# The Mixer's 128x640 turns by transposing transfers on ScalarE's queue instead of TensorE

## The chip, the cores and the metric

The kernel runs on one core of a Trainium2 chip. The metric is the device time of one execution in microseconds. Times of the kernel before come from three runs; the profile is of one execution, taken by the hardware profiler.

## The reference

Two layers are applied twice in turn to x, a sequence of 2048 tokens of width 640 (bf16): an attention layer A with recurrent memory, and a token mixer with an MLP, B.

```python
# A: for each segment of 32 tokens, with 8 memory rows in front
h = concat(mem, xs)                      # 40 x 640
q, k, v = h @ Wq, h @ Wk, h @ Wv         # 32 heads of 192
p = softmax(mask(q k^T * scale))
o = (p v) @ Wo
mem = o[:8]; out = o[8:]
# B
h  = gelu(layernorm(x) @ w1)             # 640 x 640
hs = shift the four quarters of h by +1, -1, +2, -2 tokens, @ w2
x1 = x + hs
out = x1 + gelu(layernorm(x1) @ w3) @ w4 # 640 x 1536, 1536 x 640
# the whole
x = x + A(layernorm(x)); x = x + B(layernorm(x))   # twice
```

The memory makes A serial over its 64 segments. Every weight is the same for both applications.

## The kernel before

**Tiling and stages.** Both layers run at the same time in two lanes: in step t lane 0 does segment t of the first A, lane 1 does segment t - 5 of the second (`LAG = 5`). There are 69 steps (`T_A`); steps 5 to 63 carry both lanes. A step goes through eight groups of four heads: `keys_queries` (L1707 on TensorE, copies out of PSUM at L1717, L1725, L1732), `values` or `values3` (L1754, L1781, copies L1742), `attend` (scores `fs` L1832, mask and minimum `f1` L1844, exponential L1851, sums and scaling L1855 to L1857, transposes of P L1867, copy `f5` to PT L1875, P V L1884, copy to oT L1892), and `project` (L1910). The step's result is copied from PSUM to `hT` of the next step (L1937) and, turned the feature way up, to `yTB` (`fy`, L1951, L1953). Most of the A weights are streamed from HBM in every step by SyncE (`load_pair`, L1565), the rest stay in SBUF.

**The Mixer.** B runs in 34 chunks of 64 tokens per lane, 128 rows together, a chunk over two steps: `chunk(c)` and `chunk_end(c)` belong to steps 2c + 2 and 2c + 3; the last chunk runs alone after the last step. A chunk goes through these operations, and three of them turn a 128x640 tile:

- turn one, `ft` (L2106): five TensorE transposes of `yTB` (features by tokens) into the PSUM tile `psx`; Vector adds the residual and writes `xw` (`fx`, L2111);
- LayerNorm (`ln_ops` L1964 to L1974, whose power is on GpSimd, and `apply_ln` L1980) into `vb`, which lies in the tile `vbg`;
- turn two, `transposes` (L1990): five transposes of `vb` into the PSUM tile `psv`; ScalarE copies it to `vT`, a view of `hTB` (`fe`, L2189), and four columns a second time to the end of `vT` for the lanes' neighbours (`fel`, L2192);
- w1 (L2217), GELU (`gelu`, L2008 to L2021), w2 (L2277), sums (`fs`, L2294), LayerNorm into `vb` again;
- turn three, `transposes` (L1990) and ScalarE's copy to `vT` (`fe3`, L2314);
- w3 (L2340), GELU, w4 (L2386), output `xo` (also in `vbg`, L2401) and the stores (L2425);
- `ft4` (L2440) and `fc` (L2448) hand the second A its input.

Between turn one and turn two another small product, `ftl` (L2171), prepares the next segments of the first A through the same `vb`.

**What sets the order.** Every operation is given to a planner with its engine, a cost in us, a due time and the buffers that it reads and writes (`Plan.add`). On each engine the operations stand in the order of a rank: a number from the table `RANK` for the kind of step or chunk, relative to the step's start in units of a nominal 48 us step, or, without a number there, the due time. `Plan.place` goes through the engines' lists by these ranks and its cost model, takes PSUM banks (classes A: six, B: two) and weight slots as they come free, and emits the instructions in that order; each engine's queue then runs in order, with the waits that the buffers need. A transfer's end is modelled from its size and a service rate, and SyncE's loads are also held back by the plan's time (`paced`).

Of the kernel before, what the change touches and what calls it, by code (L numbers as in the profile page):

```python
# [68 lines left out]
FLYING = 5  # L69

# [3 lines left out]
        "apply_ln.f": (390816740, 987286415, 2774608591, 3364870645,),  # L74
        "chunk.f1": (-18948399,),
        "chunk.f2": (-18747072,),
        "chunk.f3": (800691382,),
        "chunk.fe": (797633711,),
        "chunk.fe3": (3465816136,),
        "chunk.fel": (797835038,),  # L80
        "chunk.fhr": (1956035521,),
        "chunk.fhs": (3270088812,),
        "chunk.fk0": (-16266273,),
        "chunk.fk1": (1952815952,),
        "chunk.fs": (3364467992, 3364669318,),
        "chunk.ft": (18577175,),
        "chunk.ftl": (1090352636,),
        "chunk.fw": (1840327660, 1831464498, 1835801008, 3056417763, 2844233677, 2854672191, 3570130801,
            3466017462, 3490601037, 4126209402, 4046269944, 4151504855, 4600545815,),
        "chunk.fx": (31092176,),  # L90
        "chunk.fx0": (1294186538, 1072001195,),
        "chunk.fxu": (3507298104,),
# [6 lines left out]
        "load_b.fn": (-781700909, -673986775, -675212538, 1893151641, 1858630600, 1767371006, 2538152327,  # L99
            2634013608, 2675185310, 3536660548, 3527592540, 3694428291, 4147361095,),  # L100
        "transposes.f": (518350147, 3379279900,),
    },
    "chunk_0": {
        "apply_ln.f": (156241712, 835445425, 1938646249,),
        "chunk.f1": (-241661482433,),
        "chunk.f2": (-3501346185,),
        "chunk.f3": (171063840,),
        "chunk.fe": (172377420,),
        "chunk.fe3": (1969503562,),
        "chunk.fel": (172578747,),  # L110
        "chunk.fhr": (841729640,),
        "chunk.fhs": (1126117177,),
        "chunk.fk0": (941134134,),
        "chunk.fs": (1547467010, 1610110974,),
        "chunk.ft": (23776015,),
        "chunk.ftl": (171890876,),
        "chunk.fw": (256513716, 243923217, 243091367, 1428370183, 1347119499, 1346930792, 2056025287,
            1887285962, 2053039009, 2867104445, 3014371358, 2968972543, 3202475158,),
        "chunk.fx": (42023799,),
        "chunk.fx0": (367754743, 172569584,),  # L120
        "chunk.fxu": (1938774438,),
# [6 lines left out]
        "load_b.fn": (-170906047654, -170906047654, -170906047654, 920004857, 882220319, 896865883,  # L128
            1304411523, 1257239965, 1386097304, 2462708421, 2481349681, 2470811516, 2484920200,),
        "transposes.f": (164006783, 1639917844,),  # L130
    },
    "chunk_1": {
        "apply_ln.f": (3060163, 77375092, 1082267730, 1868642147,),
        "chunk.f1": (-13472039,),
        "chunk.f2": (-65645538,),
        "chunk.f3": (54909696,),
        "chunk.fe": (376700785,),
        "chunk.fe3": (2151782729,),
        "chunk.fel": (501333390,),
        "chunk.fhr": (1081898099,),  # L140
        "chunk.fhs": (2097828189,),
        "chunk.fk0": (-133135086,),
        "chunk.fk1": (993465105,),
        "chunk.fs": (1689125843, 1837451266,),
        "chunk.ft": (-11121120,),
        "chunk.ftl": (433773110,),
        "chunk.fw": (830339901, 876465320, 876266106, 1443901855, 1443901855, 1443901854, 2466889840,
            2660038962, 2340340861, 3074449991, 3356442335, 3074449991, 3363339559,),
        "chunk.fx": (-8037190,),
        "chunk.fx0": (594976846, 581135627,),  # L150
        "chunk.fxu": (2090344860,),
# [6 lines left out]
        "load_b.fn": (-1387119777, -1392412708, -1420538080, 1387323520, 1387320273, 1387321646, 1547275136,  # L158
            1584490728, 1570029792, 2481502538, 2596235860, 2552368796, 3225923724,),
        "transposes.f": (5504700, 1860426782,),  # L160
    },
    "chunk_2": {
        "apply_ln.f": (235355591, 231614731, 1557226389, 1715954030,),
        "chunk.f1": (-956916103,),
        "chunk.f2": (-402470832,),
        "chunk.f3": (394002459,),
        "chunk.fe": (316376284,),
        "chunk.fe3": (1959638099,),
        "chunk.fel": (369464748,),
        "chunk.fhr": (778257113,),  # L170
        "chunk.fhs": (1679713241,),
        "chunk.fk0": (646066165,),
        "chunk.fk1": (898552330,),
        "chunk.fs": (1715148724, 1715350050,),
        "chunk.ft": (57711930,),
        "chunk.ftl": (169733834,),
        "chunk.fw": (807022150, 806116800, 807023775, 1271841077, 1402935676, 1121619675, 2204982466,
            1956421294, 1956443760, 2937607038, 3058004067, 2968056114, 3969956053,),
        "chunk.fx": (70731042,),
        "chunk.fx0": (807216980, 804791840,),  # L180
        "chunk.fxu": (1766269180,),
# [6 lines left out]
        "load_b.fn": (-2760993007, -1565909139, -1546941875, 179913085, 793637071, 179914697, 1529941493,  # L188
            1521916561, 1529803044, 2359458277, 2313897850, 2415279936, 2436005180,),
        "transposes.f": (155739437, 1779757110,),  # L190
    },
    "chunk_end": {
        "apply_ln.f": (6227615410,),
        "chunk_end.fc": (6228018063, 6973159525, 6385136252,),
        "chunk_end.fs": (5865030923, 5870521714,),
        "chunk_end.fst": (5947665841, 6351475085,),
        "chunk_end.ft4": (6227816736,),
        "chunk_end.fw": (5037522785, 5655022894, 4980117654, 5161081694, 5762689724, 5693545930,),
        "chunk_loads.f": (5989782193, 6332049253, 6151745579, 6163156616, 6117879852,),
        "ln_ops.f1": (5947665841,),  # L200
        "ln_ops.f2": (6089632075,),
# [1132 lines left out]
def kernel(  # L1334
# [758 lines left out]
    def chunk(c):  # L2093
# [65 lines left out]
        if last:  # L2159
            warm(WARM[4], D(0.1), o0)  # L2160
# [149 lines left out]
        if last:  # L2310
            warm(WARM[12], D(0.55), o0)
# [239 lines left out]
```

## Time and profile before

| | us |
|---|---|
| median of 3 runs | 3194.13 (3189.72 to 3197.24) |
| profiled execution, first to last instruction | 3192.6 |
| TensorE busy (matmul) | 3085.9 (97%) |
| TensorE weight loads | 2758.7 (86%) |
| VectorE busy | 2050.3 (64%) |
| ScalarE busy | 1710.0 (54%) |
| GpSimd busy | 502.2 (16%) |
| granted TensorE clock, mean | 0.996 |
| moved by DMA | 859.45 MB, mean 269 GB/s |

The profiled execution's span lies inside the range of the three runs and 1.5 us below their median. "PE" is TensorE's matmul row and "PEld" its weight loads, which overlap; DVE is VectorE, ACT ScalarE, POOL GpSimd, SP SyncE. A row of groups shows line, engine, operation, what it writes and reads, how many, the busy time in us, the mean duration in ns, and how long the engine had been idle before it and for whom. Matmuls overlap, so a matmul's duration (some 220 ns for 128 columns) is not what it costs TensorE: that is the distance from one start to the next. The columns of an issue row are the size in KB and the median us from the issue to the landing.

### The profile page before, as it was taken

Reading aid. Unit: us, or ns where it says so; the run is one execution under the profiler, and the core shown is the slowest. Engines: PE = TensorE matmul, PEld = TensorE weight load, DVE = VectorE, ACT = ScalarE, POOL = GpSimd, SP = SyncE. Lnnn points to the kernel's source line nnn. Section 1 sums busy time; section 2 is a strip of 40 time slices with the busy share of each in tenths; the row PEclk is TensorE's granted clock in tenths of the full one; section 3 lists DMA queues with packets and bytes.
Section 4 is the critical chain, followed back from the end, with each engine's and each line's share of the span. In section 5 each row is a group of like instructions: output and inputs, shape, how many; then the busy total and the mean of one; then the engine's idle time right before and its main releaser. Section 6 shows DMA issues by size and latency. Waiting matters only on the chain. (4 is left out here: it accounts for less than half of the span.)

```text
span 3192.6 us, 158772 instructions
## 1 busy us (share of the span) xinstructions
PE 3085.9 (97%) x70199; PEld 2758.7 (86%) x70201; DVE 2050.3 (64%) x6448; ACT 1710.0 (54%) x3985; POOL 502.2 (16%) x983
## 2 busy tenths in 40 slices
PE   4899999999999999999999999999999999999998
PEld 3778889998888888888888889888898888888886
DVE  2666666666666666666666666666666666666675
ACT  1445555555555555565555555555555555555443
POOL 0001111111111111111111111111111111111000
PEclk8999999999999999999999999999999999999999
DMA  9888788887887887888788888877888888888786
GB/s 375 280 280 261 253 272 278 260 264 259 285 261 256 280 266 258 258 279 267 258 274 269 258 260 269 280 257 260 281 267 261 255 285 260 262 275 275 263 292 217
DMA packets 421674, 859.45 MB, mean 269 GB/s; under 512 B 48334, under 2 KB 216223, under 8 KB 420984
## 3 DMA queue, kind: packets, MB, share of 16 engines
q1 hardware_dynamic: 396776, 796.08, 75.9%
q0 software_dynamic: 24032, 53.12, 5.3%
q8 instruction: 550, 9.01, 1.2%
q14 instruction: 140, 1.15, 0.1%
q10 hardware_dynamic: 176, 0.09, 0.0%
HBM read 823.73 MB, written 25.37 MB: 266 GB/s over the span
## 5 line engine op out<-in xcount | busy, mean ns | idle before, releaser
L1707 PEld LDWEIGHTS <-wst 128*128 128x128 bf16 x19872 | 828.9, 99 | 89.4 <-issue 24.0
L1910 PE MATMUL psy<-oT,wo 128*128 128x80 bf16 (+1 forms) x16560 | 678.3, 200 | 6.9 <-issue 4.4
L1742 ACT CAST V<-psv 32x384 bf16<-32x384 f32 (+2 forms) x1032 | 478.4, 472 | 380.4 <-PE psv L1754 160.9
L1910 PEld LDWEIGHTS <-wo 128*128 128x128 bf16 x16560 | 618.0, 99 | 21.4 <-issue 19.2
L1707 PE MATMUL psk<-hT,wst 128*128 128x80 bf16 (+1 forms) x9936 | 560.6, 200 | 15.9 <-ACT hT L2448 7.1
L1707 PE MATMUL psq<-hT,wst 128*128 128x80 bf16 (+1 forms) x9936 | 541.2, 200 | 22.8 <-DMA wst<-in_A_Wq_dram 20.3
L1717 ACT CAST qT<-psq 128x480 bf16<-128x480 f32 (+1 forms) x552 | 293.6, 532 | 370.1 <-PE psq L1707 324.3
L1844 DVE CUSTOM_DVE_ANT_1 pss<-pss,mask 80x320 f32<-80x320 f32 (+2 forms) x552 | 258.5, 468 | 307.4 <-PE pss L1832 276.4
L1732 DVE CAST kT<-psk 64x160 bf16<-64x160 f32 (+1 forms) x1104 | 338.9, 307 | 93.8 <-PE psk L1707 50.8
L1892 ACT CAST oT<-pso 128x480 bf16<-128x480 f32 (+1 forms) x552 | 293.2, 531 | 176.0 <-PE pso L1884 151.2
L1851 ACT ACTIVATE Pm<-pss,sm 80x320 bf16<-80x320 f32 (+2 forms) x552 | 278.6, 505 | 162.6 <-DVE sm L1844 82.6
L1855 DVE TENSOR_REDUCE sm<-Pm 80x4 f32<-80x320 bf16 (+2 forms) x552 | 250.9, 454 | 118.9 <-ACT Pm L1851 109.6
L1875 ACT COPY PT<-pst 80x320 bf16<-80x320 bf16 (+2 forms) x552 | 220.2, 399 | 190.4 <-PE pso L1884 103.0
L1707 PE MATMUL psq<-hT,wq 128*128 128x80 bf16 (+1 forms) x6624 | 315.4, 200 | 5.8 <-issue 5.1
L1707 PE MATMUL psk<-hT,wk 128*128 128x80 bf16 (+1 forms) x6624 | 315.8, 200 | 2.1 <-issue 2.0
L1754 PEld LDWEIGHTS <-hT 128*128 128x128 bf16 x2320 | 206.5, 98 | 105.1 <-issue 1.4
L1754 PE MATMUL psv<-wv,hT 128*128 128x384 bf16 x1276 | 284.1, 326 | 0.8 <-ACT V L1742 0.8
L1857 DVE TENSOR_TENSOR Pm<-Pm,sm 80x320 bf16<-80x320 bf16 (+2 forms) x552 | 255.5, 463 | 44.3 <-PE pso L1884 0.5
L1707 PEld LDWEIGHTS <-wq 128*128 128x128 bf16 x6624 | 265.8, 99 | 17.5 <-issue 14.9
L1725 DVE CAST kT<-psk 128x320 bf16<-128x320 f32 (+1 forms) x552 | 253.4, 459 | 41.3 <-PE psk L1707 34.0
L1707 PEld LDWEIGHTS <-wk 128*128 128x128 bf16 x6624 | 266.7, 99 | 6.1 <-issue 5.8
L1762 POOL DMA_DIRECT2D vahead<-V x232 | 119.2, 515 | 954.0 <-ACT V L1742 719.5
(136 smaller groups left out, 4125.1 us busy)
## 6 DMA issues: line engine op xcount, KB each, us to landing
wst<-in_A_Wk_dram SPq DMA_DIRECT2D x556, 384.0 KB, 4.7
wst<-in_A_Wq_dram SPq DMA_DIRECT2D x556, 384.0 KB, 4.7
wstB<-in_B_w_dram SPq DMA_DIRECT2D x495, 320.0 KB, 4.5
wst<-in_A_Wv_dram SPq DMA_DIRECT2D x383, 384.0 KB, 4.9
wstB<-in_B_w_dram SPq DMA_DIRECT2D x132, 160.0 KB, 4.0
vahead<-V POOLq DMA_DIRECT2D x232, 84.0 KB, 4.2
V<-vahead POOLq DMA_DIRECT2D x232, 84.0 KB, 4.6
wo<-in_A_Wo_dram SPq DMA_DIRECT2D x8, 960.0 KB, 11.9
```

What stands on the lines that cost most here:

```text
L1707: nc.tensor.matmul(out=o[:, cc, 0:W], lhsT=wv(kc, GW * j + cc * P, GW * j + (cc + 1) * P), rhs=h[:, kc, cw:cw + W], start=begin(pq), stop= ...
L1717: nc.scalar.copy(out=qT[G % QT_BUFS][:, :, c0:c0 + N], in_=T(pq)[:, :, off:off + N])
L1725: nc.vector.tensor_copy(out=k4[:, :, 0::3, c0:c0 + N], in_=p4[:, :, 0::2, off:off + N])
L1732: copy(out=k4[r0:r1, :, jj, c0:c0 + N], in_=p4[r0:r1, :, 1, off:off + N])
L1742: (nc.vector.tensor_copy if e == "DVE" else nc.scalar.copy)(out=v_part(*dst), in_=a_)
L1754: nc.tensor.matmul(out=T(bank)[:], lhsT=left[:, kc, :], rhs=wv(kc, GWH * b, GWH * (b + 1)), start=(kc == 0), stop=(kc == KC - 1))
L1844: nc.vector.tensor_tensor_reduce(out=o, in0=o, in1=maskt.unsqueeze(1).to_broadcast([NR, HG, N]), scale=-scale, scalar=3.0e38, op0=ALU.add, ...
L1851: nc.scalar.activation(out=Pb[0:NR, :, 0:N], in_=o, func=ACT.Exp, bias=sm_[0:NR, 0:1], scale=-1.0)
L1855: nc.vector.tensor_reduce(out=sm_[0:NR, 2:2 + HG], in_=Pb[0:NR, :, 0:N], axis=AX.X, op=ALU.add)
L1857: nc.vector.tensor_tensor(out=Pb[0:NR, :, 0:N], in0=Pb[0:NR, :, 0:N], in1=sm_[0:NR, 6:6 + HG].unsqueeze(2).to_broadcast([NR, HG, N]), op=A ...
L1892: nc.scalar.copy(out=o_[:, :, off:off + N], in_=T(pso)[:, :, 0:N])
L1910: nc.tensor.matmul(out=o[:, m, cw:cw + W], lhsT=wo[:, cc, m * P:(m + 1) * P], rhs=o_[:, cc, 0:W], start=st, stop=True, skip_group_check=True)
```

## The change

In all chunks but the last, the three turns become transfers that transpose, issued from ScalarE's queue. Turn one goes from `yTB` to `vb` and Vector's add reads `vb` instead of PSUM; turns two and three go from `vb` straight to `vT`, so that the two ScalarE copies go. The copy `fel` now reads `vT` and so waits for the transfer. The last chunk stays as it was.

The planner gets a field for an operation's latency: a turn holds ScalarE's queue for `XT_HOLD` and is taken to have landed `XT_LAT2` after its start. `hTB` gets four more columns of two, the five statistics tiles become one tile, and the `RANK` tables are searched anew, at a finer unit: every order in the kernel changes. Of the tables, three rows of the new one are shown here, in units of 1/1099511627776 of the nominal us.

```diff
+XT_HOLD = 1.2
+XT_LAT = 3.0
+XT_LAT2 = 3.3
...
 RANK = {
     "chunk": {
...
-        "chunk.fe": (797633711,),
-        "chunk.fe3": (3465816136,),
...
-        "chunk.ft": (18577175,),
...
+        "chunk.fty": (-3046630172747,),
+        "chunk.fw": (14792287517455, 14867662951863, 14630708053172, 50076348630774, 49467729030636,
+            49681047132891, 59853592314991, 59856247135919, 59850937494063, 69405430859040, 60263937057968,
+            60798214861989, 72293677685014,),
...
+        "chunk.turn.fvt": (-2997552436766, 50057199061523,),
...
+        op.lat = lat
...
-        op.pr = round(67108864 * due) if k >= len(ranks) else round(67108864 * self.base) + ranks[k]
+        op.pr = round(1099511627776 * due) if k >= len(ranks) else round(1099511627776 * self.base) + ranks[k]
...
+            if o.lat:
+                done = s + o.lat
...
-    hTB = ctile([P, KC, TOK + 4, 2], bf16, "hTB")
+    hTB = ctile([P, KC, TOK + 8, 2], bf16, "hTB")
...
-    st4 = [ctile([P, 18], f32, f"st{i}") for i in range(5)]
+    st_all = ctile([P, 5 * 18], f32, "st")
+    st4 = [st_all[:, 18 * i:18 * i + 18] for i in range(5)]
...
-    nc.vector.memset(st4[4][:], 0.0)
+    nc.vector.memset(st_all[:], 0.0)
...
+        if last:
+            ps1 = ps(PB, [XB, KC, P], bf16, "psx")
+
+            def ft(op):
+                o = T(ps1)
+                for m in range(KC):
+                    nc.tensor.transpose(out=o[:, m, :], in_=yTB[:, m, 0:XB], identity=ident[:, :])
+            o0 = add("PE", mm_us(128, k=KC), D(0.05), ft, r=(B("yTB", 0), B("yTB", 1), B("fin")), w=(ps1,))
+        else:
+            def fty(op):
+                nc.scalar.dma_start_transpose(out=vb.rearrange("p (k f) -> p k f", k=KC), in_=yTB[:, :, 0:XB])
+            add("ACT", XT_HOLD, D(0.05), fty, r=(B("yTB", 0), B("yTB", 1), B("fin")), w=(vk,), dma=P * Dm * 2, lat=XT_LAT2)
 
         def fx(op):
-            nc.vector.tensor_tensor(out=xw[:], in0=T(ps1)[:].rearrange("p k f -> p (k f)"), in1=xres[:], op=ALU.add)
-        o1 = add("DVE", 0.49, D(0.05), fx, r=(ps1, B("xres")), w=(xk,))
+            in0 = T(ps1)[:].rearrange("p k f -> p (k f)") if last else vb
+            nc.vector.tensor_tensor(out=xw[:], in0=in0, in1=xres[:], op=ALU.add)
+        o1 = add("DVE", 0.49, D(0.05), fx, r=(ps1 if last else vk, B("xres")), w=(xk,))
...
+        def turn(due):
+            def fvt(op):
+                nc.scalar.dma_start_transpose(out=vT[:, :, 0:XB], in_=vb)
+            add("ACT", XT_HOLD, due, fvt, r=(vk,), w=(vTk,), dma=P * Dm * 2, lat=XT_LAT2)
+
         if last:
+            ps2 = tuple(ps(PB, [P, n_, XB], bf16, "psv") for n_ in (3, 2))
+            o0 = transposes(ps2, vb, XB, D(0.1), (vk,))
             warm(WARM[4], D(0.1), o0)
+        else:
+            turn(D(0.1))
...
-        def fe(op):
-            nc.scalar.copy(out=vT[:, :, 0:XB], in_=T(ps2)[:])
-
         def fel(op):
-            nc.scalar.copy(out=vT[:, :, XB:XB + 4], in_=T(ps2)[:, :, 0:4])
+            nc.scalar.copy(out=vT[:, :, XB:XB + 4], in_=vT[:, :, 0:4])
...
-            add("ACT", act_us(KC * XB), D(0.1), fe, r=(ps2,), w=(vTk,))
-            add("ACT", act_us(KC * 4), D(0.11), fel, r=(ps2,), w=(B("vTl"),))
+            add("ACT", act_us(KC * 4), D(0.11), fel, w=(vTk,))
...
-            add("ACT", act_us(KC * XB), D(0.55), fe3, r=(ps3,), w=(vTk,))
+            turn(D(0.55))
```

More of the change, by code (lines that the diff above doesn't have):

```diff
@@ L101 @@
-        "transposes.f": (518350147, 3379279900,),
+        "apply_ln.f": (-372675211020, 15218774534654, 47732342916953, 55180342874328,),
+        "chunk.f1": (-5297123625453,),
+        "chunk.f2": (-596251389129,),
+        "chunk.f3": (6474721953796,),
+        "chunk.fel": (8025093657600,),
+        "chunk.fhr": (23139865220247,),
+        "chunk.fhs": (45548344521130,),
+        "chunk.fk0": (-1407744258729,),
+        "chunk.fk1": (45517753037159,),
+        "chunk.fs": (48868920797077, 55126742107899,),
@@ L106 @@
[L106 to L118, printed above, removed]
@@ L160 @@
-        "transposes.f": (5504700, 1860426782,),
+        "apply_ln.f": (-8987776286037, -8986536832155, 11890397199987, 17337194053897,),
+        "chunk.f1": (-8987780203548,),
+        "chunk.f2": (-2820038147939457,),
+        "chunk.f3": (-8551644850071,),
+        "chunk.fel": (-4034404608917,),
+        "chunk.fhr": (-2686321409725761,),
+        "chunk.fhs": (16933861314027,),
+        "chunk.fk0": (-2820183299612071,),
+        "chunk.fk1": (-2753179778832609,),
+        "chunk.fs": (15076912177881, 15165530943066,),
@@ L768 @@
     },
     "start": {
[L770 to L779 removed]
+        "apply_ln.f": (-12485141366161404,),
@@ new lines @@
+        "chunk_loads.f": (-10676455869805473, -11687620307186189, -11687620307186188,),
+        "ln_ops.f1": (-12485143015423997,),
+        "ln_ops.f2": (-11687620307186190,),
+        "start.f1": (-12480908025790464,),
+        "start.f2": (-12480809814267804,),
+        "start.f3": (-12474469465651552,),
+        "start.f4": (-12485144664687195,),
+        "start.f5": (-12477688745721008, -12418499370294308, -12466767243769831, 91948283496292,),
+        "transposes.f": (-12480809814267805,),
@@ L1188 @@
     __slots__ = ("e", "d", "due", "fn", "n", "succ", "ready", "slots", "start", "end", "dma", "i", "margin",
-                 "paced", "last", "after", "mode", "pr")
+                 "paced", "last", "after", "mode", "pr", "lat")
 class Plan:
@@ L1203, in at, with add @@
         self.tag, self.base, self.seen = tag, base, {}
-    def add(self, e, d, due, fn, r=(), w=(), a=(), dma=0, queue=None, margin=0.0, after=(), mode=0, order=()):
+    def add(self, e, d, due, fn, r=(), w=(), a=(), dma=0, queue=None, margin=0.0, after=(), mode=0, order=(), lat=0.0):
         op = Op()
+        op.lat = lat
         op.mode = mode
@@ L2307, in chunk @@
         apply_ln(vb, uw, XB, st3, 0, vk, uk, s3k, D(0.5))
-        ps3 = tuple(ps(PB, [P, n_, XB], bf16, "psv2") for n_ in (3, 2)) if last else ps(PB, [P, KC, XB], bf16, "psv2")
-        o0 = transposes(ps3, vb, XB, D(0.55), (vk,))
         if last:
+            ps3 = tuple(ps(PB, [P, n_, XB], bf16, "psv2") for n_ in (3, 2))
+            o0 = transposes(ps3, vb, XB, D(0.55), (vk,))
             warm(WARM[12], D(0.55), o0)
-        def fe3(op):
-            nc.scalar.copy(out=vT[:, :, 0:XB], in_=T(ps3)[:])
-        if last:
             halves(ps3, D(0.55))
         else:
-            add("ACT", act_us(KC * XB), D(0.55), fe3, r=(ps3,), w=(vTk,))
+            turn(D(0.55))
         w3got = {}
```

1997 lines of the change are left out of this document (1137 added, 860 removed), and 150 rows, old and new, of the table RANK.

## The prediction

> **What bounds the kernel now.** I read the busy table and the window view first, then the rows of the three turns, then the order of time around two of them, then the issues of the transfers. The first two lines below are of the page, the third is the window view over one chunk (two steps) in mid-run; its columns are busy time of PE, weight loads, DVE, ACT and POOL, the granted clock, the DMA engines' share and GB/s.
>
> ```profile
> span 3192.6 us, 158772 instructions
> PE 3085.9 (97%) x70199; PEld 2758.7 (86%) x70201; DVE 2050.3 (64%) x6448; ACT 1710.0 (54%) x3985; POOL 502.2 (16%) x983
> ```
>
> ```profile
> 1585.00:1678.00 93.00, 92.47 (x2069) 83.49 (x2066) 61.70 (x192) 52.35 (x120) 17.60 (x34) 1.00 0.82 267
> ```
>
> TensorE is the bound: 92.47 of 93 us, at clock 1.00, while ACT is busy 52 of 93 us. So matmul time that goes is time gained, as long as TensorE doesn't wait for what replaces it.
>
> ```profile
> L1990 PE MATMUL psv<-ident,vbg 128*128 128x128 bf16 x340 | 30.3, 220 | 0.6 <-DVE vbg L1980 0.4
> ...
> L2189 ACT COPY hTB<-psv 128x640 bf16<-128x640 bf16 x33 | 22.9, 693 | 1.7 <-PE psv L1990 1.6
> L2314 ACT COPY hTB<-psv 128x640 bf16<-128x640 bf16 x33 | 22.8, 692 | 28.6 <-DVE xw L2305 22.2 <-PE psv L1990 6.3
> ...
> L2106 PE MATMUL psx<-ident,yTB 128*128 128x128 bf16 x170 | 15.1, 220 | 0.5 <-DVE yTB L1951 0.5
> ```
>
> The reader sees five transposes per turn, 99 turns outside the last chunk, and two ScalarE copies per chunk. (The two counts hold 5 and 10 of the last chunk.) The next rows are the order of time around turn one and turn two of one chunk (start, duration, engine).
>
> ```profile
> 1585.74 0.59 PE L1707 MATMUL psk<-hT,wst 128*128 128x80 bf16 x12 [0.26 <-ACT hT L2448]
> ...
> 1588.31 0.45 PE L2106 MATMUL psx<-ident,yTB 128*128 128x128 bf16 x5
> 1588.80 0.49 DVE L2111 TENSOR_TENSOR xw<-psx,xw 128x640 bf16<-128x640 bf16 x1 [1.39 <-PE psx L2106]
> 1589.90 0.87 DVE L1964 BATCH_NORM_STATS2 st<-xw 128x6 f32<-128x320 bf16 x2
> 1592.11 0.45 DVE L1980 TENSOR_SCALAR vbg<-xw,st 128x640 bf16<-128x640 bf16 x1 [0.44 <-POOL st L1974]
> 1592.73 0.45 PE L1990 MATMUL psv<-ident,vbg 128*128 128x128 bf16 x5
> ```
>
> The Mixer's first product (w1) starts only at 1607.93, 15 us after turn two: there was room in the chain. The third turn has none: w2 ends at 1625.35, its LayerNorm at 1628.70, the turn is at 1629.65 and w3 starts at 1631.00. What a transfer takes is seen in the issue list (KB, median us to landing).
>
> ```profile
> wst<-in_A_Wk_dram SPq DMA_DIRECT2D x556, 384.0 KB, 4.7
> wstB<-in_B_w_dram SPq DMA_DIRECT2D x132, 160.0 KB, 4.0
> h2u<-in_A_x_dram POOLq DMA_DIRECT2D x30, 80.0 KB, 2.5
> out_dram<-vbg POOLq DMA_DIRECT2D x30, 80.0 KB, 1.9
> ...
> ```
>
> **What goes.** Five transposes last 0.45 us and one 0.22, so each next one costs (0.45 - 0.22)/4 = 57 ns of TensorE. 99 turns x 5 x 57 ns = 28.2 us, all on the bound engine. About 1 us of TensorE's waits in front of these lines goes too. Sum: -29 us. [...]
>
> ScalarE loses 66 copies, 66 x 0.69 = 45.7 us, and gains 99 issues. Vector's add (0.49) reads SBUF instead of PSUM; the same operation with both inputs in SBUF (L2305) has 0.48, so nothing. The edge copy of 128x20 (0.19) stays, but now waits for the transfer. One tile for the five statistics tiles and four more columns in hTB touch only memsets at the start (under 0.4 us each): nothing. Two PSUM banks of class B lose three tiles a chunk; no wait for them is seen, so I count no gain.
>
> **What an issue and a landing cost.** The trace has no transposing transfer. The issue holds ScalarE's queue for between 0.33 us (an SP issue) and five such, 1.65 to 2.85 us (SP issues of 0.33 to 0.57), if it goes block by block. From issue to landing, L: at the least 1.7 us (0.33 plus what out_dram takes after its 0.57 us of issue, 1.33), at the most 6.5 (2.85 plus the 3.65 that the 160 KB load takes after its issue). The nearest row is the 160 KB load: the same bytes, a hardware queue, the same load on the engines, 4.0 us. A source in SBUF is worth some 0.6 less (1.9 against 2.5 for 80 KB). I take 3.4, with a spread of 0.8 both ways, since eight in ten of the weight loads behind the 4.0 landed between about 3 and 4.6. The plan itself assumes a hold of 1.2 and a landing of 3.3; that is what the order is built for, and no measurement.
>
> ScalarE's balance: 99 x 1.2 - 45.7 = +73 us, from 1710 to about 1783, 56%; at 0.33 it is -13, at 2.85 it is +236. In the window ScalarE has 40 us free per chunk, so as a sum it hides; what matters is what stands behind each issue in its queue. The 16.2 MB of the turns are 2% of 859 MB: DMA share 0.82 to about 0.84. SP issues as before, but its loads share the engines; the two long waits for weights (13.1 and 6.6 us) lie in the first 36 us, before any turn. POOL's queue loses and gains nothing; its stores of xo must now have left vbg before turn one writes it. The new ranks put those stores earlier, so nothing.
>
> **Where TensorE would wait.** The ranks fix each engine's order, so TensorE's work between two operations can be added up. As a check: by the old ranks there are 21.6 us between a chunk's first key matmul and w1, and the trace has 22.2.
>
> Turn one. By the new ranks, 23 units of six matmuls (0.215), 4 of eighteen (0.645), one value product (0.82) and one score product (0.28), 8.6 us, lie between the first key matmul and the second score product (attend.fs). That product needs a key copy which Vector runs behind the turn's consumers: add 0.49, key copy 0.31, statistics 1.37, mask 0.56, two key copies 0.66, LayerNorm 0.45, key copy 0.48, gaps 0.35 = 4.7 us. yTB is ready 0.5 us after the first key matmul. 0.55 + L + 4.7 + 0.07 = L + 5.3, against 8.6: TensorE waits for all of L beyond 3.3. Before, the turn cost 0.45 there. ScalarE stands likewise: turn two's issue waits for vb, with a query copy, the first PT copy and the second exponential behind it; the first output product needs that PT copy at 10.3 us. With a hold of 1.2 it comes at the same limit.
>
> Turn two. w1 is 15.3 us after the first key matmul, the issue at 8.0: room up to L = 7.0. The edge copy reaches the front of ScalarE's queue at about 13, so nothing waits below 5.
>
> Turn three. Between w2's end and w3 the new ranks leave 21 x 0.215 + 0.645 + 2 x 0.82 + 0.28 = 7.06 us. LayerNorm takes 3.35 (1625.35 to 1628.70 before), plus 0.1 for two semaphores: waits begin at L = 3.55. So the new order covers turns one and three up to about the planned landing of 3.3 us and no further; only turn two has room.
>
> Per chunk, with L of 2.6, 3.4 and 4.2 a third each: turn one (0 + 0.1 + 0.9)/3 = 0.33, turn three (0 + 0 + 0.65)/3 = 0.22; 0.55 x 33 chunks = 18 us. ACT and Vector run on meanwhile, so a wait for turn one is not paid again at turn two. The first chunks, where the page's first slices have the DMA engines at 0.9 and 0.8, I give 2 us more.
>
> **Sum.** 28.2 + 1 - 18 - 2 = 9 to 10 us less than the profiled execution's 3192.6 us of span, which lies 1.5 us below the median of 3194.13; the median less 10 is 3184. Half a step in L either way (0.2 us) moves this by some 7 us.
>
> **Rivals.**
> - Landings as the bulk of the weights have them, 4.2 to 4.7 us. For it: they share the engines at 0.82. Against it: ScalarE's queue has no backlog of its own. At 4.2, turn one 0.9 and turn three 0.65 (no spread): 51 us, 3194 - 29 + 51 = 3216; at 4.7, 1.4 + 1.15 = 2.55 x 33 = 84 us: 3249. It decides from L of about 3.8, where the 29 us are paid back. This is the case on the other side. Chance 0.29.
> - The gain and the waits cancel, L near 3.7 with the spread: 3188 to 3200. Chance 0.15.
> - The blocks go one after another: five issues of 0.57 and 3.65 after them, L = 6.5. Turn one 3.2, turn three 2.95, 6.15 x 33 = 203 us: 3368. For it speaks nothing in the trace but the size; chance 0.06. [...]
> - Landings of 2.6 or less: no waits, and all 29 us stay, 3165; with part of the 0.5 us a chunk that TensorE idles now in mid-run (93.00 - 92.47), 3155 to 3165. Chance 0.08.
>
> **How the numbers follow.** The likeliest case, L near 3.4, has 0.42: 3184, its own range 3165 to 3188. With the last rival it makes faster 0.50; same 0.15; slower 0.29 + 0.06 = 0.35. What a measurement here can tell from no change is 0.2%, 6.4 us. The range runs from 3160 (half of the small-L case, 0.04) to 3238 (L of 4.5: two thirds of the late-landing case, 0.19), with 0.42 and 0.15 between them: 0.80.
>
> **What would show it.** Right: the five-matmul rows of L2106 and L1990 shrink to 5 and 10 plus the start's; ScalarE's queue has three transposing issues a chunk; the issue list has 160 KB with a landing of 3 to 4 us; TensorE's waits for the mask, PT and hTB chains grow by about 0.5 us a chunk. Wrong: a median landing over 4, waits in front of w3 or of the second score product in every chunk, an issue that holds ScalarE for 2 us or more, or waits for weights in mid-run.

## The result and the profile after

The changed kernel takes 3391.69 us (median of 4 runs, 3369.08 to 3398.43), the kernel before on the same chip 3194.25 us (4 runs, 3189.72 to 3197.24). The ratio is 1.0606, 95% interval 1.0571 to 1.0641: 197 us slower, where 10 us faster was predicted and 3238 was the upper end of the range.

The first two lines are of the page of the changed kernel. The other two are the window view over some 2700 us in mid-run, in which both kernels start nearly the same number of products: first the kernel before, then the changed one (columns as in the prediction).

```profile
span 3396.7 us, 157771 instructions
PE 3137.8 (92%) x69703; PEld 2774.7 (82%) x69706; DVE 2057.8 (61%) x6448; ACT 1671.4 (49%) x3919; POOL 492.7 (15%) x983
```

```profile
300.00:2950.00 2650.00, 2625.73 (x58493) 2367.07 (x58491) 1739.80 (x5339) 1501.14 (x3396) 456.10 (x877) 1.00 0.82 267
```

```profile
310.00:3130.00 2820.00, 2675.03 (x58412) 2384.45 (x58411) 1756.98 (x5369) 1477.25 (x3358) 451.54 (x886) 0.99 0.85 257
```

TensorE has 496 products fewer, the 495 transposes among them, and takes 170 us longer over nearly as many: it was busy for all but 24 us of the first window and stood idle for 145 us of the second. The wait view of the changed kernel (total us, times, longest) says for whom, on TensorE and on Vector:

```profile
PE psh L2504 <- DMA hTB<-vbg: 65.4, 32, 5.9
PE pss L1991 <- DVE kT L1891: 51.0, 36, 3.5
...
PE pss L1991 <- DVE kT L1884: 11.7, 5, 3.0
```

```profile
DVE xw L2276 <- DMA vbg<-yTB: 57.9, 33, 5.6
DVE vbg L2336 <- DMA hTB<-vbg: 52.8, 23, 4.7
```

`psh` L2504 is w3: it waits for turn three in 32 of 33 chunks. The score products wait for key copies, and these stand on Vector behind the add of turn one (`xw` L2276), which waits 33 times for its transfer. Vector's second row is `f3`, its step of the small product `ftl`: it overwrites `vb` and so waits until turn two has read it. TensorE waits 0.6 us for it. The issue list has what the transfers took from issue to landing, which the trace before could not show, and the weights' loads beside them:

```profile
wst<-in_A_Wk_dram SPq DMA_DIRECT2D x556, 384.0 KB, 4.8
...
hTB<-vbg ACTq DMA_TRANSPOSE x66, 5.8
...
vbg<-yTB ACTq DMA_TRANSPOSE x33, 4.4
```

Here are both waits in one chunk, in order of time: turn one first, with ScalarE's issue, Vector's add and key copy, and TensorE's score product; then turn three.

```profile
1682.07 0.59 PE L1866 MATMUL psk<-hT,wst 128*128 128x80 bf16 x12 [0.26 <-ACT hT L2612]
...
1687.83 0.31 PE L1991 MATMUL pss<-kT,qT 128*128 128x80 bf16 x4
1690.09 0.30 PE L1991 MATMUL pss<-kT,qT 128*128 128x160 bf16 x2 [1.95 <-DVE kT L1891]
```

```profile
1682.22 1.22 ACTq L2271 DMA_TRANSPOSE vbg<-yTB  x1
```

```profile
1689.20 0.49 DVE L2276 TENSOR_TENSOR xw<-vbg,xw 128x640 bf16<-128x640 bf16 x1 [3.12 <-DMA vbg<-yTB]
1689.72 0.32 DVE L1891 CAST kT<-psk 64x160 bf16<-64x160 f32 x1
```

```profile
1727.94 1.22 ACTq L2324 DMA_TRANSPOSE hTB<-vbg  x1
```

```profile
1731.41 0.38 PE L1866 MATMUL psq<-hT,wst 128*128 128x80 bf16 x6
1733.25 1.56 PE L2504 MATMUL psh<-hTB,wstB 128*128 128x128 bf16 x25 [1.46 <-DMA hTB<-vbg]
```

Turn one is issued 0.15 us after the chunk's first key product and Vector can add 7 us later, the longest of the 33 (their mean is 5.0); TensorE runs out of work 1.95 us before the key copy is done. Turn three lands 5.3 us after its issue and w3 starts 1.46 us late. This chunk took 96 us where the one shown of before took 93.

To compare runs I add up TensorE's waits from the trace: of every distance between the starts of two successive products, what lies over the usual pitch of a product of its width (36 ns for 80 columns, 56 for 128; twice that where the granted clock is half, where the trace has 67 and 107), if it is more than 40 ns. "Clock" is the time lost to the granted clock by its records (in the changed kernel the mean is 0.979, and 3396.7 x 0.021 = 71). "On nothing shown" are the waits for which the trace has no releaser. All in us:

| run | span | clock | waits | on key copies | on turn three | on weights | on nothing shown | rest |
|---|---|---|---|---|---|---|---|---|
| before | 3193 | 13 | 150 | 4 | 0 | 25 | 50 | 71 |
| changed | 3397 | 71 | 329 | 82 | 71 | 34 | 39 | 103 |
| order_only | 3232 | 25 | 174 | 11 | 0 | 25 | 43 | 95 |
| nobody_waits | 3293 | 45 | 248 | 9 | 0 | 69 | 69 | 101 |
| unread_plain | 3200 | 19 | 152 | 3 | 0 | 27 | 48 | 74 |
| unread_transposing | 3236 | 21 | 187 | 6 | 0 | 30 | 81 | 70 |

From before to changed: 179 of waits, 58 of clock, less the 28 of the transposes, make 209; the spans differ by 204.

### The profile page after: what moved, and what is told of

The parts are those of the page before. It is cut to its first block, busy times and chain, and to the rows that moved or that the text cites. A ratio compares the mean times of both kernels' runs of the same rounds, so it can differ in the third digit from the quotient of the medians.

```text
span 3396.7 us, 157771 instructions
## 1 busy us (share of the span) xinstructions
PE 3137.8 (92%) x69703; PEld 2774.7 (82%) x69706; DVE 2057.8 (61%) x6448; ACT 1671.4 (49%) x3919; POOL 492.7 (15%) x983
## 3 DMA queue, kind: packets, MB, share of 16 engines
q8 instruction: 545, 8.93, 1.1%
## 4 chain that ended last, share of the span: by engine, by line
PE 69%; DMA 20%; DVE 7%; issue 2%; ACT 1%; POOL 0%; SPq 0%; DVEq 0%; POOLq 0%; ACTq 0%
PE psy L2069 15%; PE psk L1866 11%; DMA hTB<-vbg 10%; PE psq L1866 10%; PE psv L1913 10%; DMA vbg<-yTB 5%; PE pso L2043 4%; PE pss L1991 3%; PE psh L2504 3%; PE y L2550 3%; DMA wst<-in_A_Wq_dram 3%; PE psv L1940 2%; PE pst L2026 2%; PE psv L1971 2%; PE psh L2385 2%
## 5 line engine op out<-in xcount | busy, mean ns | idle before, releaser
L2069 PE MATMUL psy<-oT,wo 128*128 128x80 bf16 (+1 forms) x16560 | 692.8, 200 | 14.3 <-issue 7.4
L1901 ACT CAST V<-psv 128x384 bf16<-128x384 f32 (+3 forms) x1032 | 483.3, 475 | 405.5 <-PE psv L1913 284.3
L2069 PEld LDWEIGHTS <-wo 128*128 128x128 bf16 x16560 | 631.2, 99 | 43.1 <-issue 31.6
L1866 PE MATMUL psk<-hT,wst 128*128 128x80 bf16 (+1 forms) x9936 | 545.8, 200 | 14.1 <-ACT hT L2612 7.2
L1991 PE MATMUL pss<-kT,qT 128*128 128x80 bf16 (+2 forms) x3312 | 246.2, 211 | 67.0 <-DVE kT L1891 51.0
```

Source lines behind the costliest of these rows:

```text
L1866: nc.tensor.matmul(out=o[:, cc, 0:W], lhsT=wv(kc, GW * j + cc * P, GW * j + (cc + 1) * P), rhs=h[:, kc, cw:cw + W], start=begin(pq), stop= ...
L1901: (nc.vector.tensor_copy if e == "DVE" else nc.scalar.copy)(out=v_part(*dst), in_=a_)
L1991: nc.tensor.matmul(out=o[0:m_, i * N:(i + w_) * N].rearrange("p (a b) -> p a b", a=w_), lhsT=qTw[G % QT_BUFS][:, c * NS:c * NS + m_], rhs= ...
L2069: nc.tensor.matmul(out=o[:, m, cw:cw + W], lhsT=wo[:, cc, m * P:(m + 1) * P], rhs=o_[:, cc, 0:W], start=st, stop=True, skip_group_check=True)
```

## The experiments

**The new order without a transfer.** All three turns go back to TensorE and ScalarE in the changed kernel's order. Its table has no places for them, so the planner puts them where they can start.

```diff
-            add("ACT", XT_HOLD, due, fvt, r=(vk,), w=(vTk,), dma=P * Dm * 2, lat=XT_LAT2)
+            pt = ps(PB, [P, KC, XB], bf16, "psv")
+            transposes(pt, vb, XB, due, (vk,), True)
...
+            add("ACT", act_us(KC * XB), due, fvc, r=(pt,), w=(vTk,), fl=True)
```

> The new order with all three turns back on TensorE (five transposes and a copy out of PSUM, placed as soon as they are ready). Theory A, late landings: the 3391.7 us of the changed kernel hold waits for turn one (some 105 us in front of score products, PT and output products), for turn three (75 us in front of w3) and some 23 us of slow clock; without them, and with 28 us of transposes again, 3391.7 - 203 + 28 = about 3215, between 3190 and 3235. Theory B, the new order is slower by itself: over 3350. Theory C, the turns' packets hold up the weights and ScalarE's queue: like A, but then the waits taken away must be those for weights.

Measured: 3236.34 us (2 runs), ratio 1.013 (1.0101 to 1.016). The order alone, with the turns placed so, costs 42 us, a little over the first theory's range; the other 155 us come with the transfers.

**One turn at a time taken back.** The same, with only turn three, or only turn one, on TensorE.

```diff
-ONE_BY_DMA, TWO_BY_DMA, THREE_BY_DMA = False, False, False
+ONE_BY_DMA, TWO_BY_DMA, THREE_BY_DMA = True, True, False    # turn3_on_pe
+ONE_BY_DMA, TWO_BY_DMA, THREE_BY_DMA = False, True, True    # turn1_on_pe
```

> The changed kernel with turn three alone back on TensorE. Theory A: the 75 us in front of w3 go, with about 10 us of slow clock, and 9 us of transposes come: 3315, and the wait of the first w3 product for the transfer is gone from the list of waits. Theory B: 3391.7 + 9 = 3400.

> The changed kernel with turn one alone back on TensorE. Theory A: the 77 us of score products that wait for key copies and some 28 us behind them go, with about 12 us of slow clock, and 9 us of transposes come: 3283. Theory B: 3400. If turn two, which keeps its transfer, were the cause of those waits and not turn one, they would stay: 3380 or more.

Measured: 3314.02 us (1.0374, 1.0321 to 1.0426) and 3341.48 us (1.046, 1.0359 to 1.056). Turn three is worth 78 us, as the first theory had it; turn one 50, less than half of what it had. In each run the other turn's wait stays (w3 50.6 us without turn one; key copies 38.7 without turn three).

**What a landing takes by itself.** A program that computes nothing of the reference issues turns and single 128x128 blocks alone, then beside loads of 128 rows of 3072 bytes, then of 1280 bytes.

```diff
+    turns(12)
+    blocks(12)
+    gate()
...
+    turns(12)
+    blocks(12)
...
+    for i in range(200):
+        nc.sync.dma_start(out=slots[i % NSLOT][:], in_=src[:, i % KC, W * (i % 4):W * (i % 4 + 1)])
+    drain()
...
+    turns(12)
+    blocks(12)
+    for i in range(300):
+        nc.sync.dma_start(out=slots[i % NSLOT][:, 0:Dm], in_=src1[:, i % KC, :])
```

> No part of the reference is computed: only turns of a 128x640 tile one after another, of both shapes, and of one 128x128 block, first with nothing else moving, then beside loads of 128 rows of 3072 B, then beside loads of 128 rows of 1280 B. Theory A1, the turns' 256 B packets queue behind the weights' packets: 3.0 to 3.5 us from issue to landing alone, 5 to 7 beside rows of 3072 B, 4 to 5 beside rows of 1280 B. Theory A2, the transfer itself needs the 4.4 to 5.9 us: the same alone. One block: 1.5 to 2.5 us alone if the time goes by blocks, about that of five if not.

Measured, from the trace of one run: alone a turn holds ScalarE's queue 1.22 us and lands after 2.58, sooner than either theory had it, one block after 2.22. By the distances of the issues, each of which waits for the landing before, 20 of 24 turns take 5.1 to 8.2 us beside loads of 3072-byte rows and the other four 2.6 to 4.6; beside 1280-byte rows the median is 4.2. The windows (Vector, GpSimd, clock, DMA share, GB/s) show the other side: the loads of 3072 bytes with turns back to back beside them, the same loads without, and the loads of 1280 bytes with turns.

```profile
95.00:225.00 130.00, 0.00 (x0) 0.00 (x0) 1.00 0.71 189
280.00:380.00 100.00, 0.00 (x0) 0.00 (x0) 1.00 1.03 400
402.00:504.00 102.00, 0.00 (x0) 0.00 (x0) 1.00 0.88 216
```

So it is company that makes a landing late. And a turn of only 160 KB holds up the loads: with turns back to back the traffic falls from 400 to 189 GB/s, and of these the loads have 160.

**Transfers that nobody waits for.** The order, the issues and the traffic stay, but the three turns read a weight tile, and nothing reads what they write.

```diff
-                nc.scalar.dma_start_transpose(out=vT[:, :, 0:XB], in_=vb)
+                nc.scalar.dma_start_transpose(out=vT[:, :, 0:XB], in_=resident["k", 0][1][:, 0, 0:Dm])
...
-                                         rhs=vT[:, kc, 4:XB + 4][:, cols],
+                                         rhs=(vT[:, kc, 4:XB + 4] if last else xw[:, kc * P:(kc + 1) * P])[:, cols],
```

> The changed kernel, its order and its 99 transfers kept, but nothing waits for them: each reads a weight tile that stays in SBUF and writes vT, the add fx reads xres twice, and the w1 and w3 products of the middle chunks read xw instead of vT (so the three turns are left out of what is computed, and the output is not the reference's). Theory, the cost is the wait for late landings: 3236 of the new order with its transposes, less 28 for the transposes, so 3208 (3190 to 3235), the landings as late as before, TensorE's waits in front of the second score product and of w3 gone. Rival, the transfers cost by what they take from others (ScalarE's queue, the weights' loads): over 3300.

Measured: 3290.29 us (1.0301, 1.0274 to 1.0329): between the theories, and neither holds. The waits of w3 and of the score products are gone, but 82 us more than 3208 remain, 0.83 us for each of the 99 transfers. The table has them in waits on weights (+44 over order_only), in waits on nothing that the profile shows (+26) and in clock (+20). Not every wait for a landing is gone: ScalarE still waits for one 12 times (79 us), since turn two's issue waits until turn one has landed, and GpSimd four times. TensorE's waits under "rest" are 6 us above order_only's.

**Shorter rows.** If a turn's packets queue behind long packets of the weights, halving these helps.

```diff
-                nc.sync.dma_start(out=T(b)[:, 0:PW], in_=w_src[kind][:, kc, cols])
+                for h in range(2):
+                    c0 = PW * pr + h * PW // 2
+                    nc.sync.dma_start(out=T(b)[:, h * PW // 2:(h + 1) * PW // 2], in_=w_src[kind][:, kc, c0:c0 + PW // 2])
```

> The changed kernel with each of A's streamed weight loads issued as two, so that its rows are 1536 bytes and not 3072. Theory, a turn's 256-byte packets queue behind long weight packets: the landings fall by about 1 us (turn one to about 3.8, two and three to about 5), and with them the time by 33 x (0.9 + 1.1) = 65, to about 3325 (3280 to 3365). Rival, the landing is set by the turn's own 640 packets or by the bytes in flight: landings and time within 15 of 3392.

Measured: 3424.48 us (1.0734, 1.0696 to 1.0771), 33 us slower than the changed kernel; the issue list has 4.7 us for turn one and 6.4 for the others, more than before. Shorter packets for the weights alone do not make a turn land earlier.

**Half of the weights' bytes.** Both the order alone and the changed kernel, with half of each streamed load left out.

```diff
-                nc.sync.dma_start(out=T(b)[:, 0:PW], in_=w_src[kind][:, kc, cols])
+                nc.sync.dma_start(out=T(b)[:, 0:PW // 2], in_=w_src[kind][:, kc, PW * pr:PW * pr + PW // 2])
...
-            return T(slots[kc - nres])[:, c0:c1]
+            return T(slots[kc - nres])[:, c0 % (PW // 2):c0 % (PW // 2) + c1 - c0]
```

> The kernel of order_only (the new order, all turns on TensorE) with half of every streamed weight load of A left out: rows of 1536 bytes, and the products use the first half twice (so the output is not the reference's). Both theories: weights were not what this order waited for, so 3205 to 3240, beside the 3236 with whole loads.

> The changed kernel with half of every streamed weight load of A left out in the same way (the output is not the reference's). Theory, the turns land late because the weight loads fill the 16 DMA engines: landings fall to 3.0 to 3.8 from 4.4 to 5.9, and the time to within -30 and +25 of the run beside it that has its turns on TensorE, about 3215. Rival, the landings are the turns' own (640 packets, the issue, the completion): still 4.4 to 5.9, and 120 or more above the run beside it.

Measured: 3197.39 and 3222.0 us. The second is 25 us above the first, at the edge of what the theory allowed, instead of 155. The issue list of light_loads:

```profile
hTB<-vbg ACTq DMA_TRANSPOSE x66, 3.6
...
vbg<-yTB ACTq DMA_TRANSPOSE x33, 4.0
```

So the bytes in flight are the cause of most of the loss. They are not all of the delay: turns two and three land after 3.6 us instead of 5.8, but turn one after 4.0 instead of 4.4, later than the theory's 3.0 to 3.8, and a turn alone takes 2.6. What still delays turn one is not shown. The pair also shows that the 42 us of the order alone depend on the loads: with half of them they are not there, against what I had expected. Whether the kernel before would gain as much from lighter loads was not run.

**Turns with cover.** Can a better order pay? In two_alone only turn two goes by transfer, in the order of the kernel before with a few places moved; covered_all has all three, in an order made from that of before for the landings measured. two_alone_tensor is two_alone's order with turn two back on TensorE. Of the added lines, two_alone has the first (its `XT_LAT2` is 6.2) and covered_all all three.

```diff
-        o0 = transposes(ps2, vb, XB, D(0.1), (vk,))
+            add("ACT", XT_HOLD, D(0.1), fvt, r=(vk,), w=(vTk,), dma=P * Dm * 2, lat=6.2)
...
+            add("ACT", XT_HOLD, D(0.05), fty, r=(B("yTB", 0), B("yTB", 1), B("fin")), w=(vk,), dma=P * Dm * 2, lat=4.9)
...
+            add("ACT", XT_HOLD, D(0.55), fvt3, r=(vk,), w=(vTk,), dma=P * Dm * 2, lat=6.1)
```

> The kernel before with turn two alone by transfer, five transposes and one ScalarE copy less per chunk, and its own order changed by a few places so that w1 stands at least 6.2 us behind the issue and nothing on Vector or ScalarE that is urgent stands behind the wait. Theory 1, a landing that nobody waits for is free: the 33 x 5 x 57 ns = 9.4 us are gained, 3180 to 3195. Theory 2, each transfer costs the other loads and so TensorE some 0.9 us as in nobody_waits ((3290 - 3236 + 28) / 99 = 0.83): 33 x 0.83 - 9.4 = +18, 3205 to 3225.

> All three turns by transfer, with an order made anew from that of the kernel before for the landings that the changed kernel's trace shows (4.9, 6.2 and 6.1 us after the issue instead of 3.3), so that TensorE has other work until they land. Theory 1, late landings in an order made for 3.3 us were the cost: the waits in front of w3 and of the second score product nearly go, 3195 to 3240. Theory 2, what nobody waits for still costs some 0.83 us a transfer: 3260 to 3310.

> The order of two_alone with turn two back on TensorE, its transposes and its copy placed where they can start. Theory 1, two_alone lost its 42 us to its order: 3225 to 3245 here too. Theory 2, it lost them to the 33 transfers: 3190 to 3210 here, which would make a transfer that nobody waits for cost (42 + 9) / 33, up to 1.5 us.

Measured: two_alone 3236.12 us (1.0134, 1.0111 to 1.0156), covered_all 3306.98 (1.0356, 1.034 to 1.0372), two_alone_tensor 3198.11 (1.0028, 1.0017 to 1.0038). In covered_all the waits that the changed kernel had at w3 and at the key copies are nearly gone (2 and 17 us instead of 71 and 82), and it is still 113 us slower than before. Part of that is a new wait, for turn two, which lands later here (median 7.7 us) than the 6.2 planned:

```profile
PE psvl L1737 <- DVE vbg L1730: 36.2, 20, 5.3
```

two_alone, slower than both of its theories had it, has hardly such an excuse: TensorE waits 5 us behind turn two, in two places. Its order alone costs 4 to 8 us, by whose runs of the kernel before one compares; that leaves 34 to 38 us for its 33 transfers, and with the 9.4 us of TensorE that they save, 1.3 to 1.4 us each.

**A transfer in the old order.** The kernel before, unchanged, with 66 transfers of 128x256 behind ScalarE's two copies, into a tile that nobody reads; once transposing, once plain.

```diff
             nc.scalar.copy(out=vT[:, :, 0:XB], in_=T(ps2)[:])
+            nc.scalar.dma_start_transpose(out=un[:], in_=resident["k", 0][1][:, 0, 0:2 * P])
```

> The kernel before with its order untouched and 66 transposing transfers added, 128x256 of a weight tile that stays in SBUF, each issued from ScalarE behind a copy of turns two and three, into a tile that nobody reads. Theory 1, only waiting costs: within 6 of the kernel before (ScalarE has 40 us free a chunk, and the holds are 66 x 1.15 us). Theory 2, by transfer: 66 x 0.83 = +55; by packets (256 of a turn's 640): +22.

> The same with plain copies of 128x256 (128 rows of 512 bytes) instead of transposing transfers. If it is the transposing (its hold of ScalarE's queue, its 256-byte packets in front of the weights') that costs: within 6 of the kernel before. If any transfer more costs: as unread_transposing.

Measured: transposing 3238.11 us (1.0149, 1.0135 to 1.0162), plain 3195.28 (1.0016, 1.0003 to 1.0029), beside 3190.02 before. The transposing ones cost 48 us, 0.73 each, although they have two fifths of a turn's size and nobody waits; the plain ones 5. They land after 6.5 and 5.1 us (medians). It isn't ScalarE's queue (1.19 us of hold against 0.47): TensorE's waits on ScalarE didn't grow. What grew, by 31 of 36 us, is waiting for which the trace has no releaser. In the wait views, before and then unread_transposing ("issue" is such a wait):

```profile
PEld L1707 <- issue: 44.7, 116, 1.5
PEld L1910 <- issue: 19.2, 51, 2.4
...
PE psk L1707 <- issue: 4.8, 8, 1.4
```

```profile
PEld L1708 <- issue: 60.7, 127, 2.1
PEld L1911 <- issue: 24.3, 56, 1.5
...
PE psk L1708 <- issue: 14.5, 15, 1.8
PE psy L1911 <- issue: 8.8, 11, 1.4
```

In mid-run there are 50 such gaps of over 0.2 us, 41 us in all, where before had 22 and 12. Every one of them, in both kernels, ends 2 to 4 us after a packet of the instruction queue has started, and most of the new ones (34 of the 41 us) lie 6 to 14 us after the issue of a transfer. The queue list of the changed kernel (packets, MB, share of the 16 DMA engines) has:

```profile
q8 instruction: 545, 8.93, 1.1%
```

8.93 MB in 545 packets are 16384 bytes each. With 64 bytes for an instruction (the two instruction queues' 10.09 MB over 157771 instructions) a packet holds 256. TensorE's 139,409 products and weight loads make 545 packets: its program comes as DMA packets beside the weights, a block every 6 us.

**TensorE with nothing to wait for but its program.** Six stretches of 3200 products on fixed tiles; beside them nothing, turns, plain copies, loads of 3072-byte rows, loads and turns, loads and copies.

```diff
+    for moves in ("", "t", "p", "l", "lt", "lp"):
...
+        if "t" in moves:
+            turns(10)
+        if "p" in moves:
+            plains(10)
+        if "l" in moves:
+            loads(120)
+        stream(N)
```

> Nothing of the reference is computed: six stretches of 3200 products of 128x128 by 128x80 each on TensorE, which wait for nothing that moves; beside them nothing, 20 turns of 128x640, 20 plain copies of the same tiles, 120 loads of 128x3072 bytes, loads and turns, loads and copies. Theory: what the TensorE waits in unread_transposing without a releaser are its own instructions, which come in blocks of 16384 bytes through the same DMA engines (545 such packets in the changed kernel's trace, 8.93 MB), so the stretch with loads and turns is longer than that with loads alone by 5 us or more (20 x 0.3 to 20 x 0.8), and the others agree within 3 us. Rival, those waits come from other engines of the kernel: all six stretches within 2%.

The windows of the six stretches in that order, of one run (columns: PE, weight loads, Vector, GpSimd, clock, DMA share, GB/s):

```profile
9.60:127.80 118.20, 117.38 (x3200) 117.26 (x3200) 1.08 (x8) 0.00 (x0) 1.00 0.01 3
130.80:248.00 117.20, 116.29 (x3198) 116.19 (x3198) 1.09 (x8) 0.00 (x0) 0.99 0.16 31
251.00:368.10 117.10, 116.18 (x3200) 116.08 (x3200) 1.13 (x8) 0.00 (x0) 0.99 0.12 31
371.00:513.00 142.00, 120.61 (x3199) 118.51 (x3198) 1.17 (x8) 0.00 (x0) 0.98 0.88 335
516.00:650.80 134.80, 118.56 (x3199) 117.06 (x3199) 1.13 (x8) 0.00 (x0) 0.99 0.72 180
721.50:845.10 123.60, 117.33 (x3200) 116.69 (x3199) 1.12 (x8) 0.00 (x0) 0.98 0.82 260
```

And TensorE's order of time in the fourth:

```profile
388.29 4.75 PE L130 MATMUL ps<-rh,wt 128*128 128x80 bf16 x128 [0.92 <-issue]
394.23 4.75 PE L130 MATMUL ps<-rh,wt 128*128 128x80 bf16 x128 [1.19 <-issue]
399.89 4.75 PE L130 MATMUL ps<-rh,wt 128*128 128x80 bf16 x128 [0.92 <-issue]
```

Here TensorE waits again and again after 128 products (17 waits and 20.3 us in this stretch): with their weight loads these are 256 instructions, one block. That settles what the waits without a releaser are. Without loads the step from block to block costs no time that is seen (117 to 118 us a stretch), beside loads it does (142). But the theory's own numbers missed: loads at their full rate starve TensorE by themselves (+24 us). With turns beside them, 180 GB/s in all instead of 335, it loses 17 us, and with plain copies 6.

The last two stretches tell what it is about a turn. Here are their parts in which the transfers run, beside turns and then beside plain copies:

```profile
517.00:641.00 124.00, 110.83 (x2996) 109.63 (x2996) 0.13 (x1) 0.00 (x0) 0.99 0.72 172
733.00:818.00 85.00, 85.00 (x2374) 85.00 (x2374) 0.00 (x0) 0.00 (x0) 1.00 0.76 221
```

Beside turns TensorE waits 11 times for its program, 13.0 us together, 0.65 us a turn. Beside plain copies it doesn't wait once, although the DMA engines are a little busier and move more, and although every second copy has a turn's 640 packets of 256 bytes. So in these two parts it is the transposing that matters, and neither the share of busy engines nor the size or number of the packets; without loads turns cost TensorE nothing (the second stretch, 117.2). The two unread runs show what differs for the weights. Averaged over the 66 transfers, the weights' queue moves 282, 265, 123 and 136 GB/s in the second to fifth us after the issue of a transposing transfer, whose own packets come in the last three of these; after a plain copy it moves 283, 289, 317 and 277. By what path the program comes late when the loads are held back is not shown.

## Why the prediction was wrong

**Right.** TensorE is the bound (busy for all but 24 of 2650 us in mid-run), and 28.2 us of it went with the transposes, by the trace's pitch of 57 ns. The hold of 1.22 us (the plan's 1.2, bounds 0.33 to 2.85). The places of the waits and the limits from the ranks: turn one from a landing of 3.3 us, through Vector's add and the key copies, turn three from 3.55 in front of w3, turn two with room. With the mean landings of the changed kernel (turn one 4.75, turn three 5.91, from the 22 and 24 of 33 that the trace has) these give 1.45 x 33 = 48 and 2.36 x 33 = 78 us; taking the turns back brought 50 and 78. That these agree so closely is partly luck: taking a turn back also brings back 9 us of transposes and takes away what its 33 transfers cost by themselves, and all the waiting together is 101 us by nobody_waits, not 128. With light_loads (4.18 and 4.19) they give 29 and 21; the waits on key copies and on turn three are 23 and 18 above light_order_only's.

**Wrong: "I take 3.4, with a spread of 0.8".** The row that I held nearest was the 160 KB load at 4.0 us, and I took 0.6 off for a source in SBUF, from two rows of 80 KB (1.9 and 2.5). The same list has a third, with the source tile, the size and the queue of the 1.9:

```profile
x2d<-vbg POOLq DMA_DIRECT2D x31, 80.0 KB, 3.7
```

So the 0.6 was not the source's. The spread was read too narrow, too: of the 160 KB loads whose landing the trace has, eight in ten lie between 2.6 and 5.2 us, not between 3 and 4.6. Alone a turn would have done it in 2.6 us; in the company of the weights the rows say 4.4 and 5.8, and even the plain 64 KB of unread_plain took 5.1. In fetch_alone, beside loads, a plain copy with a turn's packets landed after 4.6 us (median), a turn after 6.1 to 6.4. The rival of late landings stopped at 4.7 and 3249.

**Wrong: no term for the rest of the new order.** I read the ranks around the turns, and the sum has nothing for what else they move. order_only has it at 42 us.

**Wrong: "DMA share 0.82 to about 0.84".** I costed the traffic by its bytes, 2%, and looked for it in the weights' waits alone. A transposing transfer that nobody waits for costs 0.7 to 1.4 us of TensorE here, so 99 of them would have eaten the 28 us more than twice over even with every landing covered. No row of the trace before prices that; but of its waits without a releaser, the 22 over 0.2 us in mid-run (12 us) all follow a packet of TensorE's program by 2 to 4 us, which could have told that this engine, too, waits for DMA traffic.

**Not foreseen: the clock.** Between 300 us and the last 250 us the records show TensorE at half clock for 3.4 or 6.8 us at a time: before had no such stretch, the changed kernel 13, of which most stand at or just behind a wait of 1.8 to 4.8 us (not every such wait has one). With the start and the end, where they are up to 17.1 us long, that is 71 us lost instead of 13. A stretch of 3.4 or 6.8 us at half clock is 1.7 or 3.4 us lost, beyond the wait in front of it.

**Small slips.** Turn three's limit adds up to 3.6, not 3.55 (4.5 + 0.65 + 1.64 + 0.28 less 3.45). ScalarE fell to 1671 and did not rise to 1783, since the profile doesn't count an issue's hold as busy (1710 - 45.7 = 1664).

In sums of runs: 42 for the order, 82 - 28 for the transfers as such (nobody_waits less order_only, 54), 101 for waiting for them (changed less nobody_waits): 197. The 82 hold the waiting that nobody_waits still has. The third rival's blocks one after another, in 6.5 us, are not what happens: alone a single block takes 2.22 and five take 2.58; the 5.8 us have another cause. Beside loads the transposing is the slower: of fetch_alone's transfers, each issued when the one before had landed, the transposing ones followed each other by 2.8 us (median) without loads and by 6.3 beside them, the plain ones by 2.5 and 4.3.

**Open.** Why the changed order loses 42 us to full loads; why a transfer cost 1.3 to 1.4 us in two_alone, 0.83 in nobody_waits and 0.73, at two fifths of the size, in unread_transposing; why the weights' queue falls to 123 and 136 GB/s behind the issue of a transposing transfer, and how that makes TensorE's program late.

## What to carry to other kernels

A transposing transfer was not priced by its bytes here: 66 of them cost this kernel 48 us where plain ones of the same bytes cost 5, and in fetch_alone they cost nothing where no loads ran (117.2 us with them, 118.2 without). Measure its landing beside the kernel's own loads, and measure once what it costs when nobody waits for it (added to the unchanged kernel, with an unread destination) before an order is built for it. TensorE's program is itself a stream (here 16 KB every 6 us), and waits without a releaser that come in units of 256 instructions, as in fetch_alone beside loads (17 of them, 20.3 us, in the fourth stretch, none in the third), say that it comes late. An order searched anew is a change of its own and needs its own run.

## What the runs showed of the hardware

- One 128x640 transposing transfer from SBUF to SBUF: 640 packets of 256 bytes (63,360 for the changed kernel's 99), 1.22 us of hold on the issuing queue, 2.58 us to landing alone (landing_alone), 4.4 to 5.8 (medians) in the changed kernel, 5.1 to 8.2 for 20 of 24 beside loads of 3072-byte rows (landing_alone).
- In landing_alone turns back to back take a load stream of 400 GB/s down to 160 (189 with their own bytes), at a DMA share that falls from 1.03 to 0.71. In unread_transposing a transfer of 64 KB takes the weights' queue from 282 GB/s to 123 and 136 in two successive us; in unread_plain nothing of the kind is seen.
- TensorE's instructions arrive in blocks of 256, as DMA packets of 16384 bytes (545 packets for 139,409 products and weight loads in the changed kernel). In fetch_alone a stream of 128x80 products lost 24 of 142 us to them beside loads of some 390 GB/s, 13.0 of 124 us beside loads and turns (172 GB/s in all), and nothing in 85 us beside loads and plain copies (221 GB/s).
- Turns land later beside the program, too: in fetch_alone's second stretch, with no loads, nine of 20 turns landed after 4.1 to 4.5 us instead of 2.6, each with a block that started 1.8 to 2.1 us after the turn's issue.
